# Attention, a routed expert layer and a gated mixing layer in one kernel: several steps moved, and two experts cut from 256 to 192 rows

## The chip, the cores and the metric

The kernel runs on one core of a Trainium2 chip. The core has five engines with a queue each: TensorE (PE; PEld in the profile is its loading of the stationary operand), VectorE (DVE), ScalarE (ACT), GpSimd (POOL) and SyncE (SP, which here only starts transfers). They wait for one another by semaphores. The metric is the device time of one execution in microseconds, the median of several.

## The reference, cut to what matters

```python
x = attention(q, k, v)        # 2 sequences of 768 rows, 8 heads of 64; a key counts when it is
                              # one of the first 8, or among the 96 up to the row itself
logits = x @ w_gate           # 8 experts
for s in rows:                # expert of a row: argmax of its logits, or, where the local gate is
    e = fresh_e if s == 0 or local_gate[s] < 0.5 else prev_e      # at least 0.5, the row before's
    out[s] = p[e] * (relu(x[s] @ w1[e]) @ w2[e])                  # 512 -> 1024 -> 512
xk = mu_k * out + (1 - mu_k) * out_prev; xr = mu_r * out + (1 - mu_r) * out_prev
y = sigmoid(xr @ w_r) * (relu(xk @ w_k) ** 2 @ w_v)               # 512 -> 1024 -> 512
```

All is float32. Which rows go to which expert is known only at run time. With the inputs used the experts get 324, 177, 166, 172, 115, 206, 96 and 280 of the 1536 rows.

## The kernel before

**Three stages.** The attention takes 12 tiles of 128 rows, in 24 iterations of four heads each (`for i in range(NI - 1)`, and the last one written out after the loop). While it runs, the routing follows it in groups of two tiles, and each row is scattered to its expert's region in memory. Then come the eight experts, one after the other, and then the mixing layer in six blocks of 256 rows.

**Products in two parts.** A weight or a row tile of the last two stages is split in a high part (a copy to a shorter number type, by ScalarE: `w_hi1`, L617) and a low part (the difference, by VectorE: `w_lo1`, L622, and `w_lo_all`, L626), and a product is three matmuls: high by high, high by low, low by high (`mm3`, L633 to L635).

**Experts by position.** The experts are sorted by their row counts at run time, and the list `PLACES` says which rank stands at which of eight positions; `CAPS` is the room of each position, `BASES` its place among the results. If an expert has more rows than its position has room, a flag is set, and the general path at the end of the kernel does everything again. Position 0 is the largest expert (two of its tiles run while the attention ends). Positions 3 and 5 (`SHORT`) are the smallest, with one tile of 128 rows and a second one behind a branch. Position 2 (`THIRD`) has two tiles of 128 and one of 64 rows. The others have two tiles of 128.

**One expert** (positions 1, 2, 4, 6). `l1m` makes the first layer: for each of eight blocks of 128 hidden columns, four steps of three matmuls with the weights as the stationary operand and the rows as the moving one (256 columns, or 320 at position 2). Two blocks share a result bank, and `relu_split` makes the high part (ScalarE) and the low part (VectorE) of the pair. `l2_mm` makes the second layer of one tile: 24 matmuls of 512 columns with the hidden rows as the stationary operand. `l2_both` does it for the 64 rows of position 2: the high and the low part stand side by side as 128 stationary columns, and 16 matmuls do, 8 with the high and 8 with the low weights; `y_both` then adds the two halves.

**Order of the work.** The order on each engine is the order of the program, written out by hand (`tc.manual_schedule`). `W_(m)` puts the next m steps of weight splitting there, `B_(m)` the next m steps of decoding the last stage's weights (three VectorE instructions for each piece, whose transfer POOL starts two buffers ahead), `next(late)` the next step of late routing (VectorE). `BL` says for each position at which of the eight blocks of the first layer a `B_` step stands, and how often one stands in the second; position 4 has steps of late routing instead.

**In the attention** an iteration is: transposes of the last iteration's weights (`emit_pT`), exponentials (`emit_exp`, ScalarE), copies of the transposes (`emit_ev`), scores of the next iterations (`emit_S`), their minima (`emit_min`, VectorE, with the tables `tb0` for each sequence's first tile and `tb` for the rest), keys and queries of the next tile (`emit_kT`, `emit_qT`), products (`emit_pv`), and on odd iterations `turn_x` and `route_x`. `at(i, point, ...)` puts routing steps at named points of an iteration. `order_a` makes a key from each expert's count so far, and `order_b` ranks the keys. From iteration 17 on `bg_early` splits the first expert's weights: each call makes the low part of the half tile whose high part the call before has made, and the high part of the next.

```python
        def bg_early():
            if ld_q:
                w_load(0, ld_q.pop(0))
            for u in lo_q[:1]:
                w_lo1(0, *lo_q.pop(0))
```

**At the start** `first_half(g)` transposes half of the first keys and queries and copies them on ScalarE (L833 and L834). `routing_consts`, at the end of iteration 1, loads the gate and sets the small constants `caps`, `bases` and `last`.

Of the kernel before, what the change touches and what calls it, by code (L numbers as in the profile page):

```python
# [16 lines left out]
P = 128  # L17
# [19 lines left out]
PLACES = (0, 1, 2, 7, 3, 6, 4, 5)  # L37
SHORT = (3, 5)
TAILED = 6
CAPS = [384, 256, 256 + LAST] + [256] * 5  # L40
# [12 lines left out]
class Net:  # L53
# [29 lines left out]
    def routing_consts(self):  # L83
# [17 lines left out]
        nc.vector.memset(self.caps, 256.0)  # L101
        nc.vector.memset(self.caps[:, 0:1], float(CAPS[0]))
        nc.vector.memset(self.caps[:, THIRD:THIRD + 1], float(CAPS[THIRD]))
        nc.vector.tensor_scalar(self.bases, self.iota_e[0:8, :], 256.0, float(BASES[3] - 768), op0=ALU.mult, op1=ALU.add)
        nc.vector.memset(self.bases[:, 0:1], 0.0)
        for r in (1, 2):
            nc.vector.memset(self.bases[:, r:r + 1], float(BASES[r]))
# [3 lines left out]
        self.last = c.tile([8, E], F32, name="last")  # L111
        nc.vector.memset(self.last, float(P))
        nc.vector.memset(self.last[:, THIRD:THIRD + 1], float(LAST))
        self.elast = None
# [237 lines left out]
    def ranks(self, pool):  # L352
# [11 lines left out]
        nc.vector.tensor_scalar(nr[:, 0, :], ep[0:1, E:2 * E], float(P), None, op0=ALU.subtract)  # L364
# [19 lines left out]
    def late_route(self, pool, big):  # L384
# [9 lines left out]
        nc.vector.tensor_scalar(nm[:, 0:1], nm[:, 0:1], -float(P), 0.0, op0=ALU.add, op1=ALU.max)  # L394
        yield
        nc.vector.tensor_tensor(b8, self.R, self.last, op=ALU.mult)
# [173 lines left out]
def build(ctx, tc, ins, out):  # L570
# [98 lines left out]
    def l2_both(r, ps, ts_):  # L669
        for f in range(KF):  # L670
            ds_ = slice((f % 2) * 512, (f % 2) * 512 + 512)
            for j, w in enumerate(whl[r, 4 + f // 2]):
                nc.tensor.matmul(ps, lhsT=ts_[f // 4][:, f % 4].rearrange("p s c -> p (s c)"), rhs=w[:, ds_],
                                 start=f + j == 0, stop=f == KF - 1 and j == 1)
            yield f
# [150 lines left out]
    def first_half(g):  # L826
# [7 lines left out]
        nc.scalar.activation(out=qz[0][:, pr, :], in_=pq, func=ACTF.Copy, scale=-1.0 / HD ** 0.5)  # L834
# [140 lines left out]
    for g in groups:  # L975
# [25 lines left out]
        if g[-1] in (5, 7):  # L1001
            e = g[-1] == 7
            at(i + 3, "Db", lambda e=e: n.order_a(ap2, "fg"[e], n.cnte if e else n.cnt6, n.fvec if e else None))
            at(*((i + 4, "Ra") if e else (i + 3, "Dc")), lambda e=e: n.order_b(ap2, "fg"[e], rp))
            at(i + 4, "Rb", lambda e=e: early_start(3 * e, e))

    with tc.manual_schedule():
# [29 lines left out]
        for _ in range(H):  # L1037
            tq.pop(0)()
# [47 lines left out]
        def bg_early():  # L1086
            if ld_q:
                w_load(0, ld_q.pop(0))
            for u in lo_q[:1]:
# [9 lines left out]
        emit_S(0)  # L1099
        first_half(1)  # L1100
        del kn[0], qn[0]
        emit_min(0)
        tq.pop(0)()
        for i in range(NI - 1):
# [40 lines left out]
            emit_min(i + 1)  # L1145
# [29 lines left out]
            if i == 4:  # L1175
                n.mix_rest()
                n.limits(n.const)
            if 0 in wsrc and early is None:
# [29 lines left out]
        emit_ev(i - 1, 0)  # L1208
        emit_ev(i - 1, 1, True)
# [10 lines left out]
        while hi_q or lo_q:  # L1220
            bg_early()
# [3 lines left out]
        oh()  # L1225
        emit_pT(i, 0)
# [61 lines left out]
    def nrow(r, i):  # L1288
        return LAST if i == 2 else P
# [12 lines left out]
    def x_hi(r, i):  # L1302
        if i == 0:
            w = 2 * P + (LAST if r == THIRD else 0)
# [22 lines left out]
    def l1m(r, f):  # L1327
# [11 lines left out]
        for kk in range(KD):  # L1339
            wh, wl = whl[r, kk]  # L1340
            xh, xl = xhl[r]
            mm3(ps, wh[:, fs], wl[:, fs], xh[:, kk, :], xl[:, kk, :], kk == 0, kk == KD - 1)
        hh, hl = (t[:, odd * 2 * P:(odd + 1) * 2 * P] for t in pair["h"])
# [247 lines left out]
    BL = {1: ((0, 0, 0, 0, 1, 0, 1, 0), 4), 2: ((1, 1, 1, 0, 1, 1, 1, 0), 3), 6: ((1, 1, 1, 0, 1, 1, 1, 0), 2)}  # L1591
# [5 lines left out]
    with tc.manual_schedule():  # L1597
# [55 lines left out]
        for r in range(1, E - 1):  # L1653
# [27 lines left out]
            for i in range(nt):  # L1681
                ps = n.bank("O", 2)
                m = nrow(r, i)
                steps = l2_both(r, ps, h3["t"]) if i == 2 else l2_mm(r, ps, i, [hs[r, f] for f in range(KF)])
                for f in steps:
# [6 lines left out]
                    elif i < 2 and f % BL[r][1] == BL[r][1] // 2:  # L1692
                        B_(1)
                if i == 2:
# [240 lines left out]
```

## Time and profile before

| | us |
|---|---|
| timed runs: median (lowest, highest) of 3 | 489.56 (489.03, 489.94) |
| profiled execution | 487.52 |
| its span, first to last instruction | 486.0 |
| TensorE busy | 468.6 |
| VectorE busy | 343.7 |
| ScalarE busy | 264.9 |
| GpSimd busy | 112.8 |
| read and written | 87.42 MB, mean 180 GB/s |

TensorE's granted clock was 0.996 of full speed. Matmuls are pipelined: the duration of one (391 ns on average for 512 columns) is longer than the time from one start to the next, so prices are taken from starts, or from a stretch divided by its count. In a row of the timeline, the bracket is how long the engine stood idle before the instruction, and what ended it. The three stages lie at about 0 to 110 us, 110 to 308 us and 308 to 486 us.

### The profile page before, as it was taken

Reading aid. Unit: us, or ns where it says so; the run is one execution under the profiler, and the core shown is the slowest. Engines: PE = TensorE matmul, PEld = TensorE weight load, DVE = VectorE, ACT = ScalarE, POOL = GpSimd, SP = SyncE. Lnnn points to the kernel's source line nnn. Section 1 sums busy time; section 2 is a strip of 40 time slices with the busy share of each in tenths; the row PEclk is TensorE's granted clock in tenths of the full one; section 3 lists DMA queues with packets and bytes.
Section 4 is the critical chain, followed back from the end, with each engine's and each line's share of the span. In section 5 each row is a group of like instructions: output and inputs, shape, how many; then the busy total and the mean of one; then the engine's idle time right before and its main releaser. Section 6 shows DMA issues by size and latency. Waiting matters only on the chain. (4 is left out here: it accounts for less than half of the span.)

```text
span 486.0 us, 9271 instructions
## 1 busy us (share of the span) xinstructions
PE 468.6 (96%) x3227; PEld 407.2 (84%) x3227; DVE 343.7 (71%) x891; ACT 264.9 (55%) x644; POOL 112.8 (23%) x198
## 2 busy tenths in 40 slices
PE   7999999799999999999999999999999999999994
PEld 5789888678788989879879888797989899898984
DVE  7777796796957866968878968797866768263301
ACT  5877876883526745576666766862433414142320
POOL 4201212112110000000000003052663918162220
PEclk9999999999999999999999999999999999999998
DMA  8996575973685887699699842102836442200001
GB/s 185 284 223 156 146 173 169 277 230 99 252 301 185 315 260 271 196 363 329 220 332 341 273 166 77 54 2 66 325 109 233 154 160 81 72 15 23 22 3 49
DMA packets 76812, 87.42 MB, mean 180 GB/s; under 512 B 50677, under 2 KB 50933, under 8 KB 76757
## 3 DMA queue, kind: packets, MB, share of 16 engines
q1 hardware_dynamic: 68304, 63.28, 41.8%
q0 software_dynamic: 4848, 16.91, 11.0%
q10 hardware_dynamic: 3604, 6.56, 3.6%
q8 instruction: 28, 0.46, 0.4%
q14 instruction: 28, 0.22, 0.1%
HBM read 73.75 MB, written 12.98 MB: 178 GB/s over the span
## 5 line engine op out<-in xcount | busy, mean ns | idle before, releaser
L617 ACT ACTIVATE whi<-wraw 128x512 fp32r<-128x512 f32 x128 | 72.5, 623 | 7.1 <-ACTq L709 2.3
L626 DVE TENSOR_TENSOR wlo<-wraw,whi 128x1024 fp32r<-128x1024 f32 x55 | 66.1, 1218 | 4.3 <-ACT whi L617 3.8
L1456 ACT ACTIVATE sq<-S 128x256 f32<-128x256 f32 x48 | 18.5, 385 | 73.1 <-PE S L635 73.1
L633 PE MATMUL S<-xkh,whi 128*128 128x256 f32 x192 | 54.3, 283 | 0.2 <-ACT whi L617 0.2
L635 PE MATMUL S<-xkh,wlo 128*128 128x256 f32 x192 | 53.3, 278 | 0.2 <-DVE wlo L622 0.2
L634 PE MATMUL S<-xkl,whi 128*128 128x256 f32 x192 | 53.2, 277 | 0.0
L1466 POOL TENSOR_TENSOR kl<-sq,kh 128x256 fp32r<-128x256 f32 x40 | 36.0, 910 | 70.0 <-issue 36.7
L1496 DVE TENSOR_TENSOR o<-O,sig 128x512 f32<-128x512 f32 (+1 forms) x13 | 8.5, 650 | 51.0 <-PE O L635 31.8
L634 PE MATMUL O<-wlo,kh 128*128 128x512 f32 (+1 forms) x104 | 39.2, 377 | 0.3 <-DVE wlo L622 0.3
L635 PE MATMUL O<-whi,kl 128*128 128x512 f32 (+1 forms) x104 | 39.2, 377 | 0.0
L633 PE MATMUL O<-whi,kh 128*128 128x512 f32 (+1 forms) x104 | 38.9, 374 | 0.0
L633 PEld LDWEIGHTS S<-xkh,whi 128*128 128x128 f32 x192 | 36.1, 188 | 0.7 <-ACT whi L617 0.4
L635 PEld LDWEIGHTS S<-xkh,wlo 128*128 128x128 f32 x192 | 36.1, 188 | 0.4 <-DVE wlo L622 0.4
L634 PEld LDWEIGHTS S<-xkl,whi 128*128 128x128 f32 x192 | 36.2, 188 | 0.3
L1457 DVE SCALAR_TENSOR_TENSOR sq<-S,sq 128x256 f32<-128x256 f32 x48 | 20.1, 420 | 15.0 <-ACT sq L1456 14.7
L1465 ACT ACTIVATE kh<-sq 128x256 fp32r<-128x256 f32 x48 | 19.7, 412 | 12.7 <-DVE sq L1457 12.7
L635 PE MATMUL O<-whi,hl 128*128 128x512 f32 x64 | 25.1, 393 | 0.0
L634 PE MATMUL O<-wlo,hh 128*128 128x512 f32 x64 | 25.1, 392 | 0.0
L633 PE MATMUL O<-whi,hh 128*128 128x512 f32 x64 | 25.0, 391 | 0.0
L278 POOL DMA_INDIRECT xs<-X,posi x12 | 12.6, 1053 | 52.8 <-DVE acc L296 20.1
L884 ACT ACTIVATE zbig<-zbig,nm 128x232 f32<-128x232 f32 (+1 forms) x48 | 22.4, 466 | 3.7 <-DVE nm L872 3.7
L634 PEld LDWEIGHTS O<-wlo,kh 128*128 128x128 f32 x104 | 19.6, 188 | 4.6 <-DVE wlo L622 0.8
(446 smaller groups left out, 1409.1 us busy)
## 6 DMA issues: line engine op xcount, KB each, us to landing
wraw<-in_moe_w_dram SPq DMA_DIRECT2D x64, 512.0 KB, 5.2
dwt<-in_moe_w_v_dram POOLq DMA_DIRECT2D x8, 512.0 KB, 4.7
z<-in_moe_w_k_dram SPq DMA_DIRECT2D x8, 512.0 KB
z<-in_moe_w_v_dram SPq DMA_DIRECT2D x8, 512.0 KB, 5.4
ys<-yo ACTq DMA_DIRECT2D x15, 256.0 KB, 6.3
xn<-xs SPq DMA_DIRECT2D x14, 256.0 KB
vn<-in_v_dram SPq DMA_DIRECT2D x12, 256.0 KB, 3.7
dwt<-in_moe_w_k_dram POOLq DMA_DIRECT2D x6, 512.0 KB, 7.6
```

The source lines that it names most:

```text
L278: self.nc.gpsimd.indirect_dma_start(self.xs, bass.IndirectOffsetOnAxis(ap=self.posi[:, t:t + 1], axis=0), X[t], None)
L617: nc.scalar.activation(out=whl[r, c][0][:, sl], in_=raws[r, c][:, sl], func=ACTF.Copy)
L626: nc.vector.tensor_tensor(lo, raws.pop((r, c)), hi.bitcast(F32), op=ALU.subtract)
L633: nc.tensor.matmul(out_, lhsT=ah, rhs=bh, start=first, stop=False)
L634: nc.tensor.matmul(out_, lhsT=ah, rhs=bl, start=False, stop=False)
L635: nc.tensor.matmul(out_, lhsT=al, rhs=bh, start=False, stop=last)
L884: nc.scalar.activation(out=pe, in_=pe, func=ACTF.Exp, scale=-1.0, bias=nm[:, h:h + 1], accum_out=sm[:, h:h + 1])
L1456: nc.scalar.activation(out=sq_, in_=ps[:, 0:TB], func=ACTF.Relu)
L1457: nc.vector.scalar_tensor_tensor(sq_, ps[:, 0:TB], 0.0, sq_, op0=ALU.max, op1=ALU.mult)
L1465: nc.scalar.activation(out=hh, in_=sq_, func=ACTF.Copy)
L1466: (nc.gpsimd if b else nc.vector).tensor_tensor(hl, sq_, hh.bitcast(F32), op=ALU.subtract)
L1496: nc.vector.tensor_tensor(o[:, a:z], ps[:, 0:z - a], sig[b, i][:, a:z], op=ALU.mult)
```

## The change

Two positions, 4 and 6 (`HALF`), get room for 192 rows: one tile of 128 and one of 64, whose second layer goes through `l2_both` and `y_both`. Their first layer has 192 moving columns, and each pair of blocks is split for the 128 and the 64 rows apart. `PLACES` puts the ranks 5, 4 and 3 at positions 4, 6 and 7 (before, ranks 3, 4 and 5). A constant `second` holds the room of the second tile, and the routing subtracts it where it subtracted 128. `BL` moves four decoding steps from position 6 to position 2, and eight steps of late routing stand in position 2's third tile.

In the attention, the copies of the first queries go from ScalarE to VectorE; four of the first tile's tables and the second half of its keys and queries come after its first minima; the small constants are set in iteration 4 instead of 1 (`place_consts`); a low part in `bg_early` waits for one more high part; the second ranking comes one iteration earlier; and the last minima come after the copy of the transposes before them.

```diff
@@ -34,10 +34,11 @@
 THIRD = 2
-PLACES = (0, 1, 2, 7, 3, 6, 4, 5)
+PLACES = (0, 1, 2, 7, 5, 6, 4, 3)
 SHORT = (3, 5)
 TAILED = 6
-CAPS = [384, 256, 256 + LAST] + [256] * 5
+HALF = (4, 6)
+CAPS = [384, 256, 256 + LAST, 256, P + LAST, 256, P + LAST, 256]
 BASES = [sum(CAPS[:i]) for i in range(E)]
@@ -98,20 +99,27 @@
         self.bases = c.tile([8, E], F32, name="bases")
-        nc.vector.memset(self.caps, 256.0)
-        nc.vector.memset(self.caps[:, 0:1], float(CAPS[0]))
-        nc.vector.memset(self.caps[:, THIRD:THIRD + 1], float(CAPS[THIRD]))
-        nc.vector.tensor_scalar(self.bases, self.iota_e[0:8, :], 256.0, float(BASES[3] - 768), op0=ALU.mult, op1=ALU.add)
-        nc.vector.memset(self.bases[:, 0:1], 0.0)
-        for r in (1, 2):
-            nc.vector.memset(self.bases[:, r:r + 1], float(BASES[r]))
         self.places = c.tile([8, E], F32, name="places")
...
         self.last = c.tile([8, E], F32, name="last")
+        self.second = c.tile([8, E], F32, name="second")
+        self.elast = None
+
+    def place_consts(self):
+        nc = self.nc
+        nc.vector.memset(self.caps, 256.0)
+        for r in (0, THIRD) + HALF:
+            nc.vector.memset(self.caps[:, r:r + 1], float(CAPS[r]))
+        nc.vector.tensor_scalar(self.bases, self.iota_e[0:8, :], 256.0, float(BASES[3] - 768), op0=ALU.mult, op1=ALU.add)
+        nc.vector.memset(self.bases[:, 0:1], 0.0)
+        for r in (1, 2) + tuple(range(HALF[0] + 1, E)):
+            nc.vector.memset(self.bases[:, r:r + 1], float(BASES[r]))
         nc.vector.memset(self.last, float(P))
         nc.vector.memset(self.last[:, THIRD:THIRD + 1], float(LAST))
-        self.elast = None
+        nc.vector.memset(self.second, float(P))
+        for r in HALF:
+            nc.vector.memset(self.second[:, r:r + 1], float(LAST))
 
@@ -361,7 +369,7 @@
         nr = pool.tile([1, 2, E], F32, name="nr")
-        nc.vector.tensor_scalar(nr[:, 0, :], ep[0:1, E:2 * E], float(P), None, op0=ALU.subtract)
+        nc.vector.tensor_tensor(nr[:, 0, :], ep[0:1, E:2 * E], self.second[0:1, :], op=ALU.subtract)
         nc.vector.tensor_tensor(nr[:, 1, :], ep[0:1, E:2 * E], self.last[0:1, :], op=ALU.subtract)
@@ -391,8 +399,11 @@
         nc.vector.scalar_tensor_tensor(nm[:, 0:1], nm[:, 1:2], self.fvec, self.cnt, op0=ALU.mult, op1=ALU.add)
-        nc.vector.tensor_scalar(nm[:, 0:1], nm[:, 0:1], -float(P), 0.0, op0=ALU.add, op1=ALU.max)
-        yield
+        yield
+        nc.vector.tensor_tensor(b8, self.R, self.second, op=ALU.mult)
+        nc.vector.tensor_reduce(nm[:, 1:2], b8, axis=AX.X, op=ALU.add)
+        yield
+        nc.vector.tensor_scalar(nm[:, 0:1], nm[:, 0:1], nm[:, 1:2], 0.0, op0=ALU.subtract, op1=ALU.max)
         nc.vector.tensor_tensor(b8, self.R, self.last, op=ALU.mult)
@@ -670,7 +681,7 @@
             for j, w in enumerate(whl[r, 4 + f // 2]):
-                nc.tensor.matmul(ps, lhsT=ts_[f // 4][:, f % 4].rearrange("p s c -> p (s c)"), rhs=w[:, ds_],
+                nc.tensor.matmul(ps, lhsT=ts_[f], rhs=w[:, ds_],
                                  start=f + j == 0, stop=f == KF - 1 and j == 1)
@@ -831,7 +842,7 @@
         nc.scalar.activation(out=strip[:, pr, 0:P], in_=pk, func=ACTF.Copy)
-        nc.scalar.activation(out=qz[0][:, pr, :], in_=pq, func=ACTF.Copy, scale=-1.0 / HD ** 0.5)
+        nc.vector.tensor_scalar(qz[0][:, pr, :], pq, -1.0 / HD ** 0.5, None, op0=ALU.mult)
         return ps
@@ -1000,8 +1011,8 @@
             e = g[-1] == 7
-            at(i + 3, "Db", lambda e=e: n.order_a(ap2, "fg"[e], n.cnte if e else n.cnt6, n.fvec if e else None))
-            at(*((i + 4, "Ra") if e else (i + 3, "Dc")), lambda e=e: n.order_b(ap2, "fg"[e], rp))
+            at(i + 3 - e, "Db", lambda e=e: n.order_a(ap2, "fg"[e], n.cnte if e else n.cnt6, n.fvec if e else None))
+            at(i + 3, "Ra" if e else "Dc", lambda e=e: n.order_b(ap2, "fg"[e], rp))
             at(i + 4, "Rb", lambda e=e: early_start(3 * e, e))
@@ -1034,7 +1045,7 @@
         first = first_half(0)
-        for _ in range(H):
+        for _ in range(4):
             tq.pop(0)()
@@ -1083,10 +1094,10 @@
 
-        def bg_early():
+        def bg_early(keep=1):
             if ld_q:
                 w_load(0, ld_q.pop(0))
-            for u in lo_q[:1]:
+            for u in lo_q[:1] if len(lo_q) > keep else ():
                 w_lo1(0, *lo_q.pop(0))
@@ -1097,10 +1108,11 @@
         emit_S(0)
+        emit_min(0)
         first_half(1)
         del kn[0], qn[0]
-        emit_min(0)
-        tq.pop(0)()
+        for _ in range(4):
+            tq.pop(0)()
         for i in range(NI - 1):
@@ -1142,7 +1154,8 @@
             bg_early()
-            emit_min(i + 1)
+            if i < NI - 2:
+                emit_min(i + 1)
             if g == 1 and i > 1:
@@ -1175,6 +1188,7 @@
                 n.limits(n.const)
+                n.place_consts()
             if 0 in wsrc and early is None:
@@ -1206,6 +1220,7 @@
         emit_ev(i - 1, 0)
+        emit_min(i)
         emit_ev(i - 1, 1, True)
@@ -1217,12 +1232,14 @@
         emit_exp(i, 1)
-        while hi_q or lo_q:
-            bg_early()
+        for _ in range(2):
+            bg_early(0)
         emit_pv(i - 1, 0)
...
         oh()
+        while hi_q or lo_q:
+            bg_early(0)
         emit_pT(i, 0)
@@ -1286,7 +1303,7 @@
     def nrow(r, i):
-        return LAST if i == 2 else P
+        return LAST if i == 2 or i == 1 and r in HALF else P
 
@@ -1301,7 +1318,7 @@
         if i == 0:
-            w = 2 * P + (LAST if r == THIRD else 0)
+            w = sum(nrow(r, j) for j in range(len(TILES[r])))
             xhl[r] = tuple(xtile([P, KD, w], c, f"x{c}{r}") for c in "hl")
@@ -1340,6 +1357,16 @@
             mm3(ps, wh[:, fs], wl[:, fs], xh[:, kk, :], xl[:, kk, :], kk == 0, kk == KD - 1)
+        if r in HALF:
+            full = pair["h"][0].rearrange("p (f s c) -> p f s c", f=2, s=2)
+            hs[r, f] = tuple(full[:, odd, j, :] for j in range(2))
+            h3[r, f] = pair["h"][1][:, odd * 2 * LAST:(odd + 1) * 2 * LAST]
+            last = pair["h"][1][:, 0:4 * LAST].rearrange("p (f s c) -> p f s c", f=2, s=2)
+            if odd:
+                both_ps = pair["ps"].rearrange("p (f c) -> p f c", f=2)
+                for t_, a, z in ((full, 0, P), (last, P, N)):
+                    relu_split(t_[:, :, 0, :], t_[:, :, 1, :], both_ps[:, :, a:z])
+            return
         hh, hl = (t[:, odd * 2 * P:(odd + 1) * 2 * P] for t in pair["h"])
@@ -1588,7 +1615,7 @@
     WS = (2, 1, 2, 1, 2, 1, 1, 1) + (2, 2, 2, 2, 2, 1, 1, 1)
-    BL = {1: ((0, 0, 0, 0, 1, 0, 1, 0), 4), 2: ((1, 1, 1, 0, 1, 1, 1, 0), 3), 6: ((1, 1, 1, 0, 1, 1, 1, 0), 2)}
+    BL = {1: ((0, 0, 0, 0, 1, 0, 1, 0), 4), 2: ((1,) * 8, 2), 6: ((1, 0, 1, 0, 0, 0, 0, 0), 2)}
     LATE = 4
@@ -1681,7 +1708,12 @@
                 m = nrow(r, i)
-                steps = l2_both(r, ps, h3["t"]) if i == 2 else l2_mm(r, ps, i, [hs[r, f] for f in range(KF)])
+                if i == 2:
+                    steps = l2_both(r, ps, [h3["t"][f // 4][:, f % 4].rearrange("p s c -> p (s c)") for f in range(KF)])
+                elif m == LAST:
+                    steps = l2_both(r, ps, [h3[r, f] for f in range(KF)])
+                else:
+                    steps = l2_mm(r, ps, i, [hs[r, f] for f in range(KF)])
                 for f in steps:
@@ -1689,9 +1721,11 @@
                         next(late, None)
-                    elif i < 2 and f % BL[r][1] == BL[r][1] // 2:
+                    elif i == 2:
+                        next(late, None)
+                    elif f % BL[r][1] == BL[r][1] // 2:
                         B_(1)
-                if i == 2:
+                if m == LAST:
                     y_both(rp, ps, BASES[r] + TILES[r][i] * P, m)
```

## Rows read from the trace of the kernel before

**Rows 1.** The page, part 1: busy time, share of the span, instructions.
```profile
PE 468.6 (96%) x3227; PEld 407.2 (84%) x3227; DVE 343.7 (71%) x891; ACT 264.9 (55%) x644; POOL 112.8 (23%) x198
```

**Rows 2.** Busy time by stretch; the columns are named in the first line.
```profile
core 0: us, PE busy (x) PEld busy (x) DVE busy (x) ACT busy (x) POOL busy (x), PEclk, DMA share, GB/s
...
10.00:20.00 10.00, 8.99 (x81) 7.06 (x79) 8.88 (x49) 9.27 (x35) 2.26 (x14) 1.00 1.11 279
...
222.20:246.00 23.80, 23.73 (x154) 21.40 (x155) 20.41 (x54) 13.46 (x26) 0.01 (x1) 1.00 0.83 278
...
259.50:282.67 23.17, 23.16 (x153) 21.20 (x153) 21.05 (x29) 13.17 (x25) 1.61 (x3) 1.00 0.92 306
```

**Rows 3.** The same: position 6's two layers, position 2's second layer and third tile.
```profile
259.51:271.68 12.17, 12.17 (x104) 12.17 (x105) 10.09 (x14) 7.68 (x15) 0.54 (x1) 1.00 0.99 339
271.70:282.67 10.97, 10.97 (x51) 9.00 (x49) 10.94 (x16) 5.48 (x10) 1.07 (x2) 1.00 0.83 269
205.05:208.70 3.65, 3.65 (x17) 3.00 (x16) 2.81 (x5) 0.60 (x1) 0.00 (x0) 1.00 0.96 345
194.05:205.04 10.99, 10.99 (x50) 9.02 (x49) 10.38 (x17) 6.65 (x15) 1.06 (x2) 1.00 0.61 178
```

**Rows 4.** Timeline of TensorE, 256 columns: first and last of ten starts.
```profile
401.73 0.28 PE L633 MATMUL S<-xkh,whi 128*128 128x256 f32 x1
...
402.75 0.28 PE L633 MATMUL S<-xkh,whi 128*128 128x256 f32 x1
```

**Rows 5.** Timeline of TensorE, 8 columns: start, duration, line, form.
```profile
122.23 0.25 PE L270 MATMUL R<-acc,tri 128*128 128x8 f32 x1
122.34 0.25 PE L268 MATMUL R<-OH,tri 128*128 128x8 f32 x1
```

**Rows 6.** Line 1323: duration in ns (least, median, largest), first and last start, forms.
```profile
L1323 DVE SCALAR_TENSOR_TENSOR hl<-S,hh x10: 418/687/693, 159.2 to 269.4; 128x512 fp32r<-128x512 f32 x6, 128x256 fp32r<-128x256 f32 x4
L1323 DVE SCALAR_TENSOR_TENSOR h3h<-S,h3h x2: 225/225/225, 182.2 to 183.9; 128x64 fp32r<-128x64 f32 x2
```

**Rows 7.** Timeline of VectorE in the attention's iterations 19 and 20.
```profile
88.24 0.69 DVE L622 TENSOR_TENSOR wlo<-wraw,whi 128x512 fp32r<-128x512 f32 x1 [1.96 <-ACT whi L617]
...
90.13 0.68 DVE L181 TENSOR_TENSOR X<-PT,RI 128x512 f32<-128x512 f32 x1
...
91.48 0.25 DVE L296 TENSOR_REDUCE acc<-OH 128x8 fp32r<-128x64 f32 x1
...
93.77 0.69 DVE L622 TENSOR_TENSOR wlo<-wraw,whi 128x512 fp32r<-128x512 f32 x1 [0.58 <-ACT whi L617]
```

**Rows 8.** Timeline of TensorE in iterations 20 and 21.
```profile
90.96 0.30 PE L891 MATMUL PT<-ident,zbig 128*128 128x128 f32 x1 [1.28 <-DVE mm L286]
...
96.29 0.20 PE L315 MATMUL R<-dgg,ones 8*8 8x8 f32 x2 [0.91 <-DVE dgg L310]
```

**Rows 9.** Waits of TensorE, 84 to 110 us: total us, times, longest.
```profile
PE O L916 <- DVE pt L902: 0.7, 1, 0.7
```

**Rows 10.** Timeline of VectorE and of ScalarE at the start.
```profile
6.07 0.38 ACT L834 ACTIVATE qz<-PT 128x256 f32<-128x256 f32 x1
...
11.94 0.07 DVE L101 MEMSET caps<- 8x8 f32 x1
...
12.52 0.40 DVE L872 CUSTOM_DVE_ANT_0 zbig<-S,tb 128x232 f32<-128x232 f32 x1
...
13.13 0.49 ACT L884 ACTIVATE zbig<-zbig,nm 128x232 f32<-128x232 f32 x1 [0.55 <-DVE nm L872]
```

**Rows 11.** Timeline of VectorE at the end of iteration 4.
```profile
24.47 0.69 DVE L902 COPY pt<-PT 128x512 f32<-128x512 f32 x1 [1.61 <-PE PT L893]
```

**Rows 12.** Groups of TensorE instructions by form: count, busy us, mean ns of one.
```profile
L195 PE MATMUL R<-wgb,xT 128*128 128x18 f32 x96 | 11.5, 261 | 0.5 <-DVE fi L334 0.5
L858 PE MATMUL T<-zbig,qz 64*128 64x232 f32 x40 | 9.4, 356 | 0.0
L268 PE MATMUL R<-OH,tri 128*128 128x8 f32 x12 | 2.6, 239 | 0.0
L858 PE MATMUL T<-zbig,qz 64*128 64x128 f32 x8 | 1.3, 285 | 0.5 <-ACT qz L834 0.5
```

## The prediction, made before the change was run

> **What bounds the kernel now.** I read the page first. TensorE is busy for 96% of the span and ScalarE and VectorE for 55% and 71% [rows 1]: TensorE sets the end unless some stage shows it waiting. The view of busy time by stage comes next, for the stretches that the edits touch [rows 2]. In the two experts that change (positions 4 and 6) TensorE is busy for 23.73 of 23.80 us and 23.16 of 23.17 us, so an instruction that goes there comes off the end. In the attention (10 to 20 us) it is busy for 8.99 of 10 us while ScalarE has 9.27 and VectorE 8.88: there the two vector engines set the pace. The rest is read from the timeline of each engine, at the gaps.
>
> **The change, part by part.** The sum is made against the profiled execution, 487.52 us: a span of 486.0 us and 1.5 us around it. The median of the timed runs, 489.56 us, is 0.4% above it, so I take the difference from the profile and put it on the median.
>
> *Two experts of 192 rows, second layer.* For a tile of 128 rows, 24 matmuls of 512 columns are issued; two tiles take 10.97 us [rows 3], so one takes 5.49 us. The tile of 64 rows puts the high and the low part side by side as 128 stationary columns and needs 16. The third tile at position 2 does this already: 3.65 us [rows 3], 228 ns each. The gain is 1.84 us per expert, **3.7 us** for both. What ends such a tile is a copy by ScalarE, then an addition by VectorE, instead of one copy; the next expert first needs a result bank after its own 24 first-layer matmuls, 5.5 us at 228 ns, so this stays hidden. The 64 rows' transfer starts from POOL's queue instead of ScalarE's, behind transfers of decoding pieces whose instructions stand earlier on VectorE too; the results are read again only after position 7's first tile, over 11 us on.
>
> *The same, first layer.* Its 96 matmuls take weights as the stationary operand and rows as the moving one, 256 columns before, 192 after. No matmul of 192 columns is in the trace. Ten of 256 columns start within 1.02 us: 113 ns each [rows 4]. Matmuls of 8 columns in the same number type start 110 ns apart when each loads 128 stationary columns [rows 5]. So loading the stationary operand costs almost as much as streaming 256 columns, and cutting columns can't go below 110 ns. Bounds by these two rows: 110 to 113 ns; I take 111, as 192 lies between, which is 2 ns for each of 192 matmuls, **0.4 us**. The stage's own 12.17 us [rows 3] with 96 matmuls and 8 transposes agrees with about 114 ns each.
>
> The Trainium skill (TensorE: Matmul & The Clock Gate, Back-to-back issue gap) gives the gap between matmuls at full clock as N/2.4 + 2.5 ns, and also says that loading weights sets the spacing with them. By the first formula alone 192 columns would take an estimated 83 ns. The rows of 8 columns speak against it here; the mechanism is rival 4.
>
> *Work on the vector engines in these experts.* Each pair of first-layer blocks had one subtraction of 512 elements on VectorE at 687 ns; it now has one of 256 (418 ns) and one of 128, between the 225 ns of 64 and those 418 [rows 6]. That is about 730 instead of 687 ns, four times: nothing against the 10 us of TensorE per layer. VectorE is full in position 6's second layer, 10.94 of 10.97 us [rows 3]. The change takes four background decoding steps out of position 6 and puts four into position 2, and moves eight steps of late routing from position 4 into position 2's third tile. Position 2's second layer has VectorE at 10.38 of 10.99 us [rows 3], so some 1 to 2 us of it will run late there, into the third tile; its weight splits end about four steps before that tile, so position 3 has its first weights in time. I cost this at nothing; with the cover gone it is 1 us. The order of positions changes which expert sits in 4, 6 and 7, not the number of tiles; the inputs give the experts there 166, 172 and 177 rows, so 192 holds.
>
> *Low parts one step later.* In the attention's iteration 19 VectorE stands for 1.96 us before a weight's low part, because ScalarE has not made the high part. The minima, the scaled row tile and the position sums queue behind it, and one iteration on it stands 0.58 us more [rows 7]. TensorE then waits 1.28 us for a transpose bank that the scaled tile frees [rows 8]. With the low part one step later no such instruction stands there, and that wait goes. One low part more (0.67 us) then lies in the tail, ahead of the last one-hot.
>
> *Keys one iteration earlier.* TensorE's wait of 0.91 us for the key [rows 8] goes, but the key's three instructions (0.6 us) now come just after the position sums, and TensorE reaches the ranking about when its transposes end. Walking the queue by the old durations, it is ready near 90.7 us and TensorE arrives near 89.9: some 0.8 us of wait comes back. Queued behind it are the ranking's three VectorE steps and then the copy of a transposed tile, which TensorE needs only after 0.95 us of other work.
>
> *Last minima later.* They stood ahead of the copy that TensorE waits for before the last but one product [rows 9]; they take 1.28 us and the copy now goes first. But the last exponentials need them, so a part comes back.
>
> The three together: of TensorE's waits 1.28 + 0.91 + 0.7 = 2.9 us go [rows 8, 9], 0.8 us comes back at the ranking and 0.3 us (half of the copy's lead) at the last exponentials; the low part that is added in the tail, 0.67 us, stands against the 0.58 us of standing that goes [rows 7]. That is **1.8 us**; the bounds are nothing (each wait comes back at the next step) and those 2.9 us.
>
> *Start.* Two query copies (0.38 us each) leave ScalarE for VectorE, and nine small constants (from 11.94 us to the minima at 12.52, 0.58 us) leave VectorE, where the minima stand behind them and ScalarE waits 0.55 us for these [rows 10]. The constants, more of them now, go where VectorE idles 1.61 us [rows 11]: hidden. But VectorE runs without a break up to these minima, and it gains 0.7 us of copies for 0.58 us of constants; the second query half now waits behind the first minima, about 0.5 us. Four tables go behind the first minima, which brings these forward 0.2 us. Bounds from 0.5 us gained to 0.6 lost; I take **0.2 us lost**, the walk's value.
>
> Sum: 3.7 + 0.4 + 1.8 - 0.2 = 5.7 us gained; less 0.2 us for small waits in position 2, **5.5 us**. On the profile 482.0 us, on the median **484.1 us**.
>
> **Rivals.**
> 1. *The experts gain, the attention doesn't* (its waits turn into others: three of the four edits put work on VectorE's path elsewhere). For it: VectorE has 8.88 of 10 us at the start. Against it: the 1.28 us wait has one clear cause. 3.9 gained, 0.6 lost: 486.3 us.
> 2. *Fewer than 256 moving columns cost what plain float32 costs.* All weight matmuls of this type have 256 columns or more now, so nothing shows 192. A plain one is two instructions (96 records for 48 matmuls of 18 columns), and at 128 and 232 columns these take 285 and 356 ns, 0.68 ns per column [rows 12]: 192 columns twice are 262 ns, 149 more than now, for 192 matmuls 28.6 us lost against 5.1 gained elsewhere: 513 us, slower. Against it: at 8 columns the type is still one instruction [rows 12] and starts each 110 ns. It decides once a matmul of 192 columns takes over 140 ns (5.1 us over 192 matmuls, above 113).
> 3. *VectorE or the weight transfers bind in the shorter experts.* The transfers' share is 0.83 in position 4 and 0.92 in position 6 [rows 2], and VectorE is full in position 6. Against it: among ScalarE's waits there none is for a transfer. If it takes the experts' 4.1 us, and with rival 1 the tail's gain is gone too: 489.6 us, no change.
> 4. *The spacing follows the columns.* 228 ns for 512 and 113 for 256 columns are 0.45 ns each more [rows 3, 4], so 192 would take 84 ns and the first layers gain 29 ns in 192 matmuls, 5.6 us instead of 0.4: 478.9 us. Against it: the 110 ns of 8 columns [rows 5].
>
> That the change doesn't do what it says would need an expert of over 192 rows at 4 or 6, and the general path; the counts exclude it.
>
> **How the numbers follow.** The forecast 0.70, rival 1 0.13, rival 2 0.10, rival 3 0.04, rival 4 0.03. A measurement of this kernel tells about 0.2%, 1 us, from no change. Faster: 0.70 + 0.13 + 0.03 = 0.86; the same 0.04; slower 0.10. The forecast's own range adds the ends: 2.5 to 4.2 us from the experts, 0 to 2.9 from the tail, 0.6 lost to 0.5 gained at the start, so 1.9 to 7.6 us gained, 482.0 to 487.7 us. With rival 1 and a part of rival 3 it reaches 488.0; rivals 2 and 4 are left out: 481.6 to 488.0.
>
> **What would show it.** In the changed trace: 16 matmuls of `l2_both` at the end of each of positions 4 and 6, in 3.65 us, and first-layer starts 110 to 113 ns apart for 192 columns; starts of 140 ns or more make me wrong. The wait for the transpose bank near 90 us is gone and the ranking's wait is under 0.9 us. The first minima of the second tile start near 12.7 us. If TensorE's idle time in positions 3 to 7 is more than 1 us longer than before, rival 3 holds.

## The result, and the profile after

The changed kernel takes **494.38 us** (median of 4 runs, 494.28 to 496.17) against 489.75 us before (4 runs, 489.03 to 490.16): the ratio is 1.0114, 95% interval 1.0083 to 1.0145. It is slower by 4.6 us where 5.5 us of gain were forecast, and the range (481.6 to 488.0) misses it.

The profiled execution took 496.17 us, its span is 494.4 us. The page's first part, answering [rows 1]: TensorE is busy 2.9 us longer with 16 instructions fewer; its mean granted clock was 0.983, where it had been 0.996.

```profile
PE 471.5 (95%) x3211; PEld 408.3 (83%) x3211; DVE 344.9 (70%) x913; ACT 265.2 (54%) x650; POOL 113.7 (23%) x200
```

I cut the span at the first matmul of each position in TensorE's timeline, and the mixing layer's at its first product with `xkh` (so the first block's two products with `w_r` count to position 7):

| us | attention, position 0 | 1 and 2 | 3 | 4 | 5 | 6 | 7 | mixing layer |
|---|---|---|---|---|---|---|---|---|
| before | 154.94 | 53.77 | 13.51 | 23.78 | 13.51 | 23.16 | 30.88 | 172.49 |
| after | 156.84 | 53.77 | 22.67 | 21.31 | 15.00 | 20.80 | 31.03 | 172.97 |
| difference | +1.90 | 0.00 | **+9.16** | -2.47 | +1.49 | -2.36 | +0.15 | +0.48 |

The two changed experts gain 4.8 us, more than the 4.1 forecast. Position 3, in which not one instruction was changed, loses 9.2 us.

Busy time by stretch (columns as in [rows 2]): the start, position 2's second layer and third tile, TensorE's stall in position 3, and positions 4 and 6 (6 in its two layers, and then its tile of 64 rows alone).

```profile
core 0: us, PE busy (x) PEld busy (x) DVE busy (x) ACT busy (x) POOL busy (x), PEclk, DMA share, GB/s
10.00:20.00 10.00, 9.46 (x76) 7.73 (x75) 8.50 (x40) 8.30 (x32) 2.28 (x17) 0.83 1.16 241
195.95:206.95 11.00, 11.00 (x50) 9.02 (x49) 10.23 (x17) 6.96 (x16) 1.05 (x2) 1.00 0.57 185
206.95:210.61 3.66, 3.66 (x17) 3.00 (x16) 1.54 (x2) 0.60 (x1) 0.53 (x1) 1.00 0.86 283
217.40:226.27 8.87, 2.04 (x5) 1.38 (x5) 7.99 (x26) 2.16 (x4) 1.10 (x2) 0.74 0.54 170
233.28:254.59 21.31, 21.31 (x146) 19.52 (x147) 16.41 (x42) 11.77 (x27) 0.00 (x0) 1.00 0.74 239
269.59:281.20 11.61, 11.61 (x105) 11.61 (x105) 8.75 (x14) 7.61 (x17) 0.56 (x1) 1.00 0.98 355
281.20:290.39 9.19, 9.19 (x42) 7.54 (x41) 8.81 (x14) 5.54 (x11) 0.54 (x1) 1.00 0.77 239
286.73:290.39 3.66, 3.66 (x17) 3.00 (x16) 3.66 (x6) 1.75 (x3) 0.54 (x1) 1.00 0.97 312
```

Against [rows 3], position 6's second layer has gone from 10.97 to 9.19 us and its first from 12.17 to 11.61. In position 2's third tile VectorE works 1.54 of 3.66 us, where it worked 2.81: it has more to do there than before, and stands.

192 columns, TensorE's timeline (answers [rows 4]): seven starts in 0.78 us, 111 ns each. By the formula that the Trainium skill (TensorE: Matmul & The Clock Gate, Back-to-back issue gap) gives for the gap at full clock, N/2.4 + 2.5 ns, it would be an estimated 83 ns; the trace decides.

```profile
233.56 0.27 PE L646 MATMUL S<-xh,wlo 128*128 128x192 f32 x1
...
234.34 0.27 PE L644 MATMUL S<-xh,whi 128*128 128x192 f32 x1
```

Where the 9.2 us go is read from three engines' queues. VectorE first (start, duration, line, and in brackets the idle time before and what ended it):

```profile
206.67 0.69 DVE L501 SCALAR_TENSOR_TENSOR z<-dwt,z 128x512 uint32<-128x512 uint32 x1
207.28 1.22 DVE L637 TENSOR_TENSOR wlo<-wraw,whi 128x1024 fp32r<-128x1024 f32 x1
213.04 0.43 DVE L497 TENSOR_SCALAR z<-dwt 128x512 uint32<-128x512 uint32 x1 [4.54 <-DMA dwt<-in_moe_w_v_dram]
...
215.24 0.69 DVE L501 SCALAR_TENSOR_TENSOR z<-dwt,z 128x512 uint32<-128x512 uint32 x1
217.72 0.43 DVE L497 TENSOR_SCALAR z<-dwt 128x512 uint32<-128x512 uint32 x1 [1.79 <-DMA dwt<-in_moe_w_v_dram]
218.07 0.15 DVE L395 TENSOR_TENSOR b<-Rr,bases 8x8 f32<-8x8 f32 x1
...
220.80 0.67 DVE L753 TENSOR_TENSOR yo<-O,yo 64x512 f32<-64x512 f32 x1
221.41 2.34 DVE L637 TENSOR_TENSOR wlo<-wraw,whi 128x1024 fp32r<-128x1024 f32 x2
223.67 0.67 DVE L658 TENSOR_TENSOR ehl<-PT,ehh 128x512 fp32r<-128x512 f32 x1
```

L497 is the first of a piece's three decode steps, L501 the last. VectorE stands 4.54 and 1.79 us for a piece's transfer; before the change none of its waits in positions 2 and 3 was for one. Behind these steps in its queue stand the late-routing steps (from 218.07), the third tile's result, two weights' low parts, and `ehl`, the low hidden part of position 3. POOL's timeline shows when the transfers were started:

```profile
198.51 0.53 POOL L769 DMA_DIRECT2D dwt<-in_moe_w_v_dram  x1 [8.06 <-DVE zbig L501]
204.86 0.53 POOL L769 DMA_DIRECT2D dwt<-in_moe_w_v_dram  x1 [5.82 <-DVE z L501]
207.65 0.53 POOL L769 DMA_DIRECT2D dwt<-in_moe_w_v_dram  x1 [2.27 <-DVE z L501]
216.22 0.53 POOL L769 DMA_DIRECT2D dwt<-in_moe_w_v_dram  x1 [8.04 <-DVE z L501]
```

Each waits for an L501, because there are two buffers and the last step of a piece frees one. The transfers' own time, from issue to landing (the view of transfers, one row for each of three windows), is 4.7 us for the one started at 198.51, and 8.2 and 10.0 us for the next two:

```profile
dwt<-in_moe_w_v_dram POOLq DMA_DIRECT2D x1, 512.0 KB, 4.7
...
dwt<-in_moe_w_v_dram POOLq DMA_DIRECT2D x1, 512.0 KB, 8.2
...
dwt<-in_moe_w_v_dram POOLq DMA_DIRECT2D x1, 512.0 KB, 10.0
```

So position 2 takes steps faster than two buffers can be refilled, and the last of its steps stand for transfers that land 8 and 10 us after their start. TensorE's timeline shows the price:

```profile
217.17 0.40 PE L645 MATMUL O<-wlo,ehh 128*128 128x512 f32 x1
224.40 0.79 PE L646 MATMUL O<-whi,ehl 128*128 128x512 f32 x1 [6.83 <-DVE ehl L658]
224.99 0.63 PE L644 MATMUL O<-whi,ehh 128*128 128x512 f32 x1
225.42 0.63 PE L645 MATMUL O<-wlo,ehh 128*128 128x512 f32 x1
225.84 0.63 PE L646 MATMUL O<-whi,ehl 128*128 128x512 f32 x1
```

6.83 us idle, and then starts 0.42 us apart where full clock gives 0.23: after the idle time the granted clock is 0.50, the lower of TensorE's two levels (1.2 GHz), until 228.4 us:

```profile
224.40:228.40 4.00, 4.00 (x13) 3.42 (x14) 2.71 (x3) 0.78 (x2) 0.00 (x0) 0.50 0.97 334
```

In this stretch it starts five matmuls of 512 columns and eight transposes, which take 1.9 us at full clock (0.23 and 0.09 us each): some 2 us more of the 9.2.

The second stall is in position 5: TensorE waits 1.1 us for `ha5h`, and ScalarE's waits point to a reason, an exponential of late routing (L462) before which it stood 3.7 us in its queue, with casts of weights behind it. (Before the change it stood 2.7 us there, and TensorE did not wait.) First the row of TensorE, then that of ScalarE:

```profile
PE PT L654 <- ACT ha5h L668: 1.1, 1, 1.1
...
ACT pex L462 <- DVE pex L461: 3.7, 1, 3.7
```

The attention: the bank wait of 1.28 us [rows 8] and the copy's 0.7 us [rows 9] are gone, and of the key's 0.91 us 0.68 stays:

```profile
93.06 0.19 PE L323 MATMUL R<-dgg,ones 8*8 8x8 f32 x2 [0.68 <-DVE dgg L318]
```

Yet it ends 1.9 us later in this profile. The first minima of the second tile start at 14.47 us, where they started at 12.52 [rows 10], and the granted clock is 0.83 at 10 to 20 us and 0.72 at 100 to 105, where the first profile had 1.00. Whether that is the change is for the experiments.

### The profile page after: what moved, and what is told of

Same layout as the page of the kernel before. It is cut to its first block, busy times and chain, and to the rows that moved or that the text cites. A ratio compares the mean times of both kernels' runs of the same rounds, so it can differ in the third digit from the quotient of the medians.

```text
span 494.4 us, 9267 instructions
## 1 busy us (share of the span) xinstructions
PE 471.5 (95%) x3211; PEld 408.3 (83%) x3211; DVE 344.9 (70%) x913; ACT 265.2 (54%) x650; POOL 113.7 (23%) x200
## 5 line engine op out<-in xcount | busy, mean ns | idle before, releaser
L646 PE MATMUL O<-whi,ehl 128*128 128x512 f32 x40 | 16.5, 412 | 6.8 <-DVE ehl L658 6.8
L644 PEld LDWEIGHTS O<-whi,kh 128*128 128x128 f32 x104 | 19.6, 188 | 3.7
L646 PEld LDWEIGHTS O<-whi,kl 128*128 128x128 f32 x104 | 19.6, 188 | 3.6
```

Source lines behind the costliest of these rows:

```text
L644: nc.tensor.matmul(out_, lhsT=ah, rhs=bh, start=first, stop=False)
L646: nc.tensor.matmul(out_, lhsT=al, rhs=bh, start=False, stop=last)
```

## The experiments

Two theories were open. **D**: VectorE stands at decode steps for transfers that came too late. **A**: the loss is in the attention. Medians are of one chip in each group of four, and the kernel before was timed on it too (490.28, 490.06 and 489.91 us in e, f and g).

| kernel | us | ratio to before, 95% interval |
|---|---|---|
| e1, decode table as before | 488.60 | 0.9971 (0.9956 to 0.9985) |
| e2, experts' edits alone | 495.80 | 1.0126 (1.0082 to 1.0171) |
| e3, attention's edits alone | 487.92 | 0.9954 (0.9939 to 0.9968) |
| e4, no late routing in position 2 | 494.63 | 1.0098 (1.0073 to 1.0122) |
| f1, position 2's steps as before | 489.89 | 1.0006 (0.9978 to 1.0034) |
| f2, and four steps in position 4 | 488.42 | 0.9983 (0.9956 to 1.0011) |
| f3, and the exponential later | 488.00 | 0.9971 (0.9952 to 0.9990) |
| f4, and the old start | 487.28 | 0.9968 (0.9945 to 0.9991) |
| g1, the best in one | 488.15 | 0.9958 (0.9933 to 0.9983) |
| g2, attention alone, old start | 488.65 | 0.9982 (0.9961 to 1.0002) |
| g3, decode without its transfers | 488.28 | 0.9981 (0.9956 to 1.0007) |

### e1: the decode table as before

```diff
-    BL = {..., 2: ((1,) * 8, 2), 6: ((1, 0, 1, 0, 0, 0, 0, 0), 2)}
+    BL = {..., 2: ((1, 1, 1, 0, 1, 1, 1, 0), 3), 6: ((1, 1, 1, 0, 1, 1, 1, 0), 2)}
```

> The changed kernel, with only the table of decode steps as before: position 2 takes 7 + 4 steps (not 8 + 8), position 6 takes 6 + 8 (not 2 + 8). Theory D (VectorE stands in its queue at a decode step for a word-weight transfer that was started only when the buffer came free, and TensorE behind it): the 6.8 us stall of position 3 on ehl is gone and with it the half clock behind it, 494.4 - 8 = 486 us (484.5 to 488.5), clock back to about 0.99. Theory A (the loss is in attention: later start, lower clock): position 3 gains, something later takes it back, 492 to 494. Theory L (the eight late-routing steps in position 2's third tile hold the queue): the stall stays at 4 us or more, 491 to 494.

(A slip in it: by the code, position 2 took 6 + 6 steps before, not 7 + 4.) Two rows of one table are worth some 6 us: 488.60 us against the changed kernel's 494.38, which is from another group of runs (by the ratios 1.4%, 7 us). That is 0.1 above D's range and over 2 us from the rivals'. Position 3 is back at 13.65 us. What D had not said: position 7 is now 1.8 us longer (32.67 us), with a stall on the same tile. TensorE's and VectorE's waits there:

```profile
PE O L646 <- DVE ehl L658: 1.5, 1, 1.5
...
DVE z L497 <- DMA dwt<-in_moe_w_v_dram: 1.2, 1, 1.2
```

So a shorter position 6 can't hold 14 steps: moving some out was needed, and position 2 was the wrong place for them.

### e2 and e3: the two halves of the change

e2 is the changed kernel with every hunk of the attention undone, e3 the kernel before with these hunks alone:

```diff
-        nc.scalar.activation(out=qz[0][:, pr, :], in_=pq, func=ACTF.Copy, scale=-1.0 / HD ** 0.5)
+        nc.vector.tensor_scalar(qz[0][:, pr, :], pq, -1.0 / HD ** 0.5, None, op0=ALU.mult)
...
+            at(i + 3, "Ra" if e else "Dc", lambda e=e: n.order_b(ap2, "fg"[e], rp))
...
+            for u in lo_q[:1] if len(lo_q) > keep else ():
```

> The changed kernel with all edits of the attention undone (scaled query copy on ScalarE, order of the first tables and minima, place constants at the beginning, low parts, keys and last minima where they were); the expert part as changed. Theory D: the stall of about 6.8 us in position 3 stays, 492 to 495 us. Theory A: the loss was in attention, so 486 to 489. If both are at work: about 490 to 492.

> The kernel before with the edits of the attention alone; experts and decode steps as before. Theory D: no loss here; by the prediction's term -1.8 + 0.2 it is 488.1 us, with the start of the changed profile at most 1 us above the kernel before: 487.5 to 490.8. Theory A: 491 to 493, with the first expert's products 1.5 us or more later than in the kernel before.

e2 keeps a stall of 6.2 us in position 3 and is the slowest of all; e3 is 2.4 us faster than its kernel before. A falls: the loss is in the experts' half. By the ratios the two halves add up to +0.80%, against +1.14% for the whole change, which their intervals allow.

### e4: late routing back in position 4

```diff
-                    elif i == 2:
-                        next(late, None)
-                    elif f % BL[r][1] == BL[r][1] // 2:
+                    elif i < 2 and f % BL[r][1] == BL[r][1] // 2:
```

> The changed kernel without the eight late-routing steps in position 2's third tile (they run in position 4, as before); decode steps as changed. Theory D: VectorE still stands at the decode step for its transfer (4.5 us) but has 2.3 us less to do behind it, so the stall of position 3 shortens by about 2.3 us and no more: 491 to 493 us. Theory L: the stall is gone or under 2 us, 486 to 489.

The stall shrinks to 3.5 us, by 3.3 where D said 2.3, and L is out: VectorE stands for transfers as long as in the changed kernel (6.1 us in two waits; there 6.3). So about half of the stall is the late steps that stand in the queue behind the wait. But the median is the changed kernel's, not 491 to 493. Position 4, with all late steps again and less time for them, is 23.22 instead of 21.31 us, with a TensorE wait of 1.8 us on VectorE's L421; position 5, without its wait for `ha5h`, is 13.75 instead of 15.00. The profiled execution is the fastest of the four (492.02 us), and its positions 3 to 7 together are 2.9 us shorter than the changed kernel's; why the other three show nothing of it stays open.

### f1 to f4: a place for the four steps

f1 sets `BL` for position 2 as before and for 6 as changed. f2 adds a place, f3 puts the exponential three places later than the subtraction that feeds it:

```diff
                     if r == LATE:
-                        next(late, None)
+                        if next(late, 0) == 0 and f % 2:
+                            B_(1)
...
         nc.vector.tensor_tensor(ex, self.LS[:, :, 0:E], self.MX.unsqueeze(2)...)
+        yield
+        yield
+        yield
         nc.scalar.activation(out=ex, in_=ex, func=ACTF.Exp)
```

> The changed kernel with position 2's decode steps as before (12 in its first layer and first two second-layer tiles, not 16) and position 6's as changed (10, not 14); the four steps left over come where the rest is drained, between position 7's two tiles. Theory Q (what matters is whether VectorE stands before a low hidden part of a position with one 128-row tile when TensorE wants it): position 3's stall on ehl 1.5 us or less, as in the kernel with both rows as before, and the 1.8 us of that kernel in position 7 on the same tile gone; 488.6 - 1.8 = 486.8 us, up to 488.3 if the four drained steps (4 x 0.69 us) take it back. Theory N (no more than four steps matter, wherever they stand): 488 to 489 with 1.5 to 2 us of new stall at the drain.

(The stall of 1.5 us that it speaks of was in position 7, not in 3.) f1 missed: 489.89 us lies above Q's range and N's, and the new stall is the one that N had said. Position 3 is 13.66 us here, so position 2's row of the table alone makes its stall. The steps left over run in position 7, and VectorE stands there for transfers again, 3.7 us in two waits; position 7 is 33.62 us:

```profile
PE O L646 <- DVE ehl L658: 2.2, 2, 1.2
...
DVE z L497 <- DMA dwt<-in_moe_w_v_dram: 3.7, 2, 2.3
```

> As the kernel before this one, and the four left-over decode steps in position 4's second tile of the second layer, whose places are empty since eight late-routing steps moved to position 2. Theory Q: no stall over 0.5 us in position 7 and none at the drain, but position 4 ends with VectorE behind, so position 5's stall of 1.1 us on ha5h stays: 486 to 487 us. Rival: VectorE runs late in position 4 already (ScalarE waited 3.7 us there for pex), the four steps lengthen position 5's stall to 2 us or more: 487.5 to 489.

488.42 us is in the rival's range, but the stall is the one of Q. Position 7 is 30.95 us, without a stall over 0.2 us; position 5 keeps its 1.1 us and is 0.7 us longer (15.73).

> As the kernel before this one, and ScalarE's exponential of the routing scores is put three places later than the subtraction that it needs. Theory E (ScalarE stands 3.7 us in its queue before that exponential for VectorE, and the casts of weights and ha5h behind it are late): position 5's stall of 1.1 us on ha5h goes to under 0.3, another 1 us off: 485 to 486. Rival S (ScalarE has more to do than the shorter second layer of position 4 leaves time for): the stall stays at 0.8 us or more and the time is that of the kernel before this one.

E is right on the wait and wrong on the gain. TensorE's wait on `ha5h` is gone from the list of positions 4 and 5; what is left there is

```profile
PE O L649 <- DVE ehl L661: 0.3, 1, 0.3
```

but position 5 is 14.82 us: 0.9 us better than in f2, 0.2 better than after, and 1.3 us above before. TensorE's next block, the one that needs `ehh` and `ehl`, takes 2.27 us for 1.38 us of matmuls. Position 7, where nothing was edited, is 0.6 us longer in this profile (31.57 us), which leaves 0.3 of the 0.9. The time, 488.0, is the rival's.

f4 undoes the edits of the start, but for the small constants:

```diff
-        nc.vector.tensor_scalar(qz[0][:, pr, :], pq, -1.0 / HD ** 0.5, None, op0=ALU.mult)
+        nc.scalar.activation(out=qz[0][:, pr, :], in_=pq, func=ACTF.Copy, scale=-1.0 / HD ** 0.5)
...
-        for _ in range(4):
+        for _ in range(H):
             tq.pop(0)()
...
         emit_S(0)
-        emit_min(0)
         first_half(1)
         del kn[0], qn[0]
-        for _ in range(4):
-            tq.pop(0)()
+        emit_min(0)
+        tq.pop(0)()
```

> As the kernel before this one, with the start as in the kernel before the change: the scaled query copy on ScalarE, all eight first tables ahead, the first minima after the second half, one table after it. By the prediction's term the new start costs 0.2 us (bounds -0.5 to +0.6), so this is 0.2 us faster than the kernel before this one; by the changed profile (each of the first two score products waits 0.6 to 1.2 us on VectorE's query copy, where it waited 0.5 on ScalarE's) it is 0.6 to 1.2 us faster; if the start is caught up by 100 us, equal within 0.2.

487.28 us, in the median 0.7 less than f3, but by the ratios 0.03%, and g2 against e3 shows the other sign. The start's worth isn't settled. In position 7 TensorE waits 1.0 us for `ehl` again (32.18 us), with the decode steps where f2 had no such wait.

### g1 to g4

g1 is f4 with two of the three `yield` lines and the four steps at places 2 to 5 (`if next(late, 0) == 0 and 1 < f < 6`). g2 is e3 with f4's diff. g4 is the kernel before. g3 leaves the transfers of pieces out:

```diff
+            held = dw[i]
             yield from dec(i, word_tile)
             for j in PIECES[TAILED + k_ + 2:TAILED + k_ + 3]:
-                dec_load(j, dw_tile())
+                dw[j] = held
```

> The changed kernel, all decode steps where the change puts them, but only the first two of the fourteen word weights are transferred behind the first expert and every later decode reads the older buffer (the later weights are left out, so the result is another). Theory D (VectorE stands for a transfer, not for the work of the steps): the stall of 6.8 us on ehl in position 3 falls to 1.5 us or less, 486 to 489 us. Rival V (VectorE has too much work in position 2, whose end it reaches late): the stall stays at 5 us or more, 493 to 495.

This is the decisive one. All 16 steps are in position 2, with the same work for VectorE; without transfers the stall falls from 6.8 to 0.3 us, the time by 6.1 us (6.5 by the ratios), and none of VectorE's waits in positions 2 and 3 is for a transfer. Of TensorE's waits in positions 2 to 5 two are left:

```profile
PE PT L654 <- ACT ha5h L668: 1.1, 1, 1.1
PE O L646 <- DVE ehl L658: 0.3, 1, 0.3
```

V falls. (Fewer transfers also leave more room for the weights'; how much of the 6.1 us that is wasn't taken apart.)

> All that helped so far in one kernel: the changed kernel with the start as before, position 2's decode steps as before, the four left-over steps in position 4's second tile (places 2 to 5), ScalarE's exponential two places later. By the stage lengths of the single profiles (155 us to the end: 331.1 us in the kernel before, 329.2 to 329.5 in the three best variants), and the attention's -2.3 us in time: 490.1 - 2.3 - 1.8 = 486 us. If the experts' edits are worth nothing on the clock, it equals the next kernel within 0.3 us.

> The kernel before with the attention edits except those of the start (low parts, keys, constants and last minima moved; scaled query copy and first tables as before); experts as before. Difference to the kernel ahead of this one is the experts' net worth in its best arrangement: by the prediction -4.1 us, by the stage lengths -1.8, by rival Z (given back elsewhere) 0. Against the kernel before: by the prediction's terms -1.8, so 488.3; with the start's 0.5 us gained over the earlier attention-only kernel 487.4.

g1 is 488.15 us and misses its 486; g2 is 488.65 us. By the ratios the experts' edits are worth 0.24%, 1.2 us, in their best place, with overlapping intervals; in the profiles positions 4 to 7 take 88.28 us in g1 and 91.24 in g2, and why the timed runs show less than these 3 us stays open. e3, g1, f4, f3 and e1 are faster than the kernel before, by 0.3 to 0.5%, each with an interval below 1; no order among them can be told.

> The kernel before once more, for a second profile. Theory K (the first profile is the rarer kind of execution, without a fall of TensorE's granted clock in the attention): this one has a clock of 0.8 to 0.9 somewhere in 78 to 105 us and is 489 to 490.6 us, its experts (155 us to the end) as long as in the first profile within 0.5 us. Otherwise: clock 1.00 throughout there and 487 to 488 us.

489.47 us, with the fall of the clock that K said (from 155 us on it is 0.7 us shorter than the first profile, not within 0.5). In this profile the granted clock is 0.83 at 80 to 90 us, in e3 0.66 at 100 to 105:

```profile
80.00:90.00 10.00, 9.64 (x86) 8.50 (x86) 5.75 (x26) 6.02 (x20) 0.47 (x3) 0.83 1.02 299
```
```profile
100.00:105.00 5.00, 4.97 (x45) 4.16 (x45) 4.39 (x17) 2.95 (x10) 0.00 (x0) 0.66 0.89 276
```

The first profile of before was of the rarer, shorter kind: of its 35 runs in the second group 31 took 489.07 to 490.64 us and 4 took 487.15 to 487.98. That the clock makes the difference isn't shown: the mean granted clock is 0.996 or more in the 4, but in 13 of the 31 too. The attention and position 0 take 154.9 to 157.1 us in three profiles without the edits and 154.9 to 158.8 in eleven with the new ones (three of them with the old start): a single profile can't tell the edits' gain. The timed runs can: -2.4 us in e3; in g2 it is -0.9 by its ratio, with an interval that reaches no change. The 1.9 us of the comparison above lie within this spread. So does the start: the minima that began at 14.47 us after the change begin at 12.9 to 13.2 in six of the seven other profiles with the new start, with a clock of 1.00 at 10 to 20 us in all seven.

## Why the prediction was wrong

**The step that failed** is "Work on the vector engines in these experts", and in it "I cost this at nothing; with the cover gone it is 1 us". In the sum it stands as 0.2 us "for small waits in position 2"; it came to 9.2 us in position 3. It counted VectorE's work: four steps of 0.4 to 0.7 us, against busy time in position 2. What binds is the transfer that each third step needs, and two buffers allow no more than two of them ahead. Four steps of about 0.6 us, put where they use up the two buffers faster than these are refilled, cost some 6 us (after against e1): VectorE stood 6.3 us, all that was queued behind it stood too (the late-routing steps are 3.3 of the stall's 6.8 us, by e4), and TensorE then ran at half clock. g3 shows that it is the transfer. The prediction saw VectorE running late "into the third tile" and looked for who needs the weights next; `ehl`, the tile that TensorE needs first from VectorE in position 3, it did not look for.

**Second layer, 3.7 us, and first layer, 0.4 us.** Right in their place: 16 matmuls of `l2_both` in 3.66 us in both positions, 111 ns for 192 columns, positions 4 and 6 shorter by 2.47 and 2.36 us; position 6's first layer gave 0.56 us for the 0.2 forecast. But 1.5 us came back in position 5. The likely reason is that ScalarE and VectorE have less time behind position 4's shorter second layer: in e4, where position 4 takes 1.9 us longer, the wait is gone. f3 moves the wait and doesn't remove it. The sum of positions 4 to 7 is 3.2 us less than before. So the 5.5 us would not have come without the stall either: the best arrangement, g1, gains 0.42%, 2.1 us, against the kernel before.

**The split** of 256 and 128 elements takes medians of 417 to 425 and 291 to 292 ns, together 708 to 717 where about 730 were forecast:

```profile
L1340 DVE SCALAR_TENSOR_TENSOR hh<-S,hh x4: 424/425/425, 236.6 to 278.9; 128x256 fp32r<-128x256 f32 x4
L1340 DVE SCALAR_TENSOR_TENSOR hl<-S,hl x4: 290/292/292, 237.4 to 279.7; 128x128 fp32r<-128x128 f32 x4
```

**The attention, -1.8, and the start, +0.2**, together -1.6: timed -2.4 (e3). Two waits went as forecast, and 0.68 us of the key's stayed against 0.8. The sum lies within the bounds; but for the start its parts were not run one by one, and g2, without the new start, gives only -0.9. So it is not shown that these terms made the gain: the clock that falls at 80 or at 100 us was in none of them. The sign given for the start, minima near 12.7 us, failed in the profile after (14.47); in most others with the new start they begin at 12.9 to 13.2.

**The rivals.** Rival 3 (VectorE or the weight transfers bind) had the mechanism and 4% of the chance. Its place was the experts that shrink and its price their gain; it struck one position after the one that took the steps. By the prediction's own mark, over 1 us of idle time in positions 3 to 7, it holds: 7.9 us. Rivals 2 and 4 are out at 111 ns, rival 1 by e3 (less clearly by g2). That the difference was put on the median and not on the profile was right: the profile lay 2 us below it.

## What to carry to other kernels

Before an instruction that reads a transferred buffer is moved earlier, walk its buffers: which instruction frees one, how long the transfer behind it takes there under load, and how many buffers lie between; with that, n steps can be had for nothing only if their transfers could have started. Then name what stands behind it in the same queue, down to the first tile that the bounding engine needs. And take a second profile of the baseline, since one execution may be of the rarer kind.

## What was not expected of the hardware

A 512 KB transfer from POOL's queue took 4.7 us from issue to landing, and 8.2 and 10.0 us a few microseconds later, beside the weights' transfers. After 6.83 us of idle time TensorE's granted clock was 0.50 and its 512-column starts were 0.42 us apart until 228.4 us; then they were 0.23 apart again. In the attention the granted clock falls to 0.50 at 80 to 81 us in five of the fourteen profiles, at 100 to 103 us in eight, and in one not at all; why stays open.
